# The second layer's w_in operands kept in DRAM as f32, and split into high and low parts after they are loaded

## The chip, the cores and the metric

The kernel runs on one core of one Trainium2 chip. The metric is device time in microseconds (us), the median of three runs. The engines are named as in the profile: PE (TensorE, the matmuls), PEld (its weight loads), DVE (VectorE), ACT (ScalarE), POOL (GpSimd), SP (SyncE, which here only issues DMA transfers).

## The reference, cut to what matters

Three stages follow each other: an attention over chunks of 32 queries, an MLP with softplus, and an MLP with PReLU, whose slope `alpha` is a vector over the 2048 hidden units. All is in float32.

```
a   = softmax(scale * q_c @ k_full.T)      # 24 chunks of 32 queries, 4 batches, 8 heads
x   = (a @ v_full)                         # laid out as 3072 tokens x 512
h   = x @ moe_w_in                         # 512 x 2048
x   = (relu(h) + log1p(exp(-|h|))) @ moe_w_out
h   = x @ moe2_w_in
out = (relu(h) + alpha * min(h, 0)) @ moe2_w_out
```

## The kernel before, in words

Matmuls run on f32r operands. To keep the accuracy of f32, each operand is split: the high part is a cast by ACT (`act.copy` into an f32r tile), the low part is the difference of the operand and its high part. A product is then three matmuls: high by high, high by low, low by high. In each group of three, the first two use the high part of the weight; the third alone uses its low part. The second alone uses the low part of the moving operand.

**First layer and attention.** Here every step of every engine is a piece with a cost, a due time and rooms that it takes and gives back. The class `Plan` orders the pieces for each engine, eight times over with refined due times, and the best order is written out. `raw` weights come in as 64-bit words, DVE turns them into f32 (`magnitude`, `clamp`, `convert`), and the second layer's weights are prepared along the way: for each q of 8, `weight_sums` lets POOL form four sums, then the seven operands (A11, A12, A22, S1 to S4, each 128x256) are split by ACT and POOL in a staging room (`wst`) and stored to DRAM by SP, high and low parts, in `in_ops`. Operands for w_out go the same way to `out_ops`.

**Second layer.** Three pairs of token blocks (p = 0, 1, 2) follow each other. A pair has eight quads (`quad`, q = 0 to 7), which compute h with seven products instead of eight, and then 56 groups (`second`, n = 0 to 55), which multiply by w_out. A quad has 42 matmuls in the order A11, S1, S2, S3, A12, S4, A22; a group has six. Each quad reads two rooms of `win`, loaded by `load_w_in` two quads ahead, behind the quad's last product. ACT and DVE take the products out of PSUM: copies c1 and c5 (tile `tc`), sums (`u`, `ps_q`, `gb`), the PReLU (`tp`, then `gb`). In the 56 groups, `ready` makes the moving operand `g`: a cast by ACT, a subtraction by DVE, three groups ahead at the end. The engines' queues are in program order. Rooms of `win` are shared with others (tag "w", 16 rooms).

At the end of the 56 groups, `second` loads the operands of the next pair's first two quads, one room each at 12, 8, 4 and 1 groups before the end; `flip` transposes results and stores them by four DMAs for each half.

Of the kernel before, what the change touches and what calls it, by code (L numbers as in the profile page):

```python
# [7 lines left out]
F32 = mybir.dt.float32  # L8
F32R = mybir.dt.float32r
I32 = mybir.dt.int32  # L10
AF = mybir.ActivationFunctionType
ALU = mybir.AluOpType
# [4 lines left out]
P = 128  # L17
DM, DFF = 512, 2048
# [32 lines left out]
NPAIRS = NB // 2  # L51
# [125 lines left out]
def attention_mlp_mlp_kernel(ctx: ExitStack, tc, qk, v, w1, w2, consts, out):  # L177
# [22 lines left out]
    ident = cst[:, :P]  # L200
    alpha_sb = cst[:, P:]
    y_dram = dpool.tile([DM, NTOK], F32, name="y_dram")
    in_ops = dpool.tile([NQ, P, 2, 7, HK], F32, name="in_ops")
    out_ops = dpool.tile([7, 2, P, NQ // 2, 2, HK], F32, name="out_ops")


# [90 lines left out]
        pool.tensor_tensor(out=t[:, 2, :], in0=a11, in1=a21, **sub)  # L297
        pool.tensor_tensor(out=t[:, 3, :], in0=a12, in1=t[:, 1, :], **sub)

    def operands_at(q, second, k, n):  # L300

        if second:
            return [out_ops[k + e, q // 4][:, q % 4] for e in range(n)]
        return [in_ops[q][:, :, k:k + n, :].rearrange("p a k n -> p a (k n)")]


    raw_q, q_t, k_t, v_t, st, s_room = {}, {}, {}, {}, {}, {}
# [264 lines left out]

    y_raw, x_op, w_in, w_out, slots, G, g2 = {}, {}, {}, {}, {}, {}, {}

    def switch_pools():
        early.close()
# [35 lines left out]
        t, x = y_raw.pop((p, h, k)), x_op[p, k][:, :, h, :]  # L614
        dve.tensor_tensor(out=x[:, 1, :], in0=t, in1=x[:, 0, :].bitcast(F32), op=ALU.subtract)

    def load_w_in(n, part=(0, 1)):
        if n >= NPAIRS * NQ:
            return
        p, q = divmod(n, NQ)  # L620
        for a, b in [((0, 4), (4, 7))[e] for e in part]:
            t = wpool.tile([P, 2, b - a, HK], F32R, tag="w", name="win")
            sp.dma_start(out=t.bitcast(F32), in_=in_ops[q][:, :, a:b, :])
            for k in range(a, b):
                w_in[n, k] = t[:, :, k - a, :]


    PASSES = ((S1, T1, 1), (A11, B11, 0), (S4, B22, 3), (S2, T2, 1), (S3, T3, 0), (A12, B21, 2), (A22, T4, 1))
# [51 lines left out]
    def plus(out, in0, in1, op=ALU.add):  # L680
        dve.tensor_tensor(out=out, in0=in0, in1=in1, op=op)
# [3 lines left out]
    def quad(p, q, between, ahead):  # L685


        n, f0, f1 = p * NQ + q, 2 * q, 2 * q + 1
        if q % 4 == 0:
            for k in range(4):  # L690
                room = (wpool if k else xpool).tile([P, 4, N2], F32, tag="w" if k else "x", name="gb")
                slots[k, q // 4] = room
                for e in range(4):
                    G[k, q + e] = room[:, e, :]
        banks = [("acc", ps_acc)] * 4 if q % 2 else [("pa", ps_a), ("h", ps_h)] * 2
        x1, x4, x3, x2 = (bank(space, tag) for tag, space in banks)
# [12 lines left out]
        ahead(2)
        n3 = negative(G[3, q], f1)  # L710
        between()
        product(p, n, A12, B21, x1, False)
        n0 = halves_of(x1, G[0, q])
        ahead(3)
        product(p, n, S4, B22, x4, False)
        prelu(G[3, q], n3, G[3, q])
        plus(G[1, q], x4, u2)
        minus_prelu(n0, f0, G[0, q])
        if q < NQ - 1:
            n1 = negative(G[1, q], f0)  # L720
        product(p, n, A22, T4, x3, False)

        def second_rest(n1):
            prelu(G[1, q], n1, G[1, q])
            dve.scalar_tensor_tensor(out=G[1, q], in0=G[1, q], scalar=-1.0, in1=G[0, q], op0=ALU.mult, op1=ALU.subtract)
        if q < NQ - 1:
            second_rest(n1)
            n2 = halves_of(x3, G[2, q])
            minus_prelu(n2, f1, G[2, q])
        else:  # L730
            third = []
            rest[:] = [
                lambda: second_rest(negative(G[1, q], f0)),
                lambda: third.append(halves_of(x3, G[2, q])),
                lambda: minus_prelu(third[0], f1, G[2, q]),
            ]
        if q < NQ - 2:
            load_w_in(n + 2)
        else:
            for k in range(2):  # L740
                load_w_out(14 * p + 2 * (q - NQ + 2) + k)

# [40 lines left out]
    def second(p, todo):  # L783
# [34 lines left out]
        for n in range(7 * NQ):  # L818
            i, q = divmod(n, NQ)
            ka = PASSES[i][0]  # L820
            w = w_out[14 * p + n // 4][:, n % 4]
            if q == 0:
                ps = ps_of[ka] = [bank(*spaces[ka]) for _ in range(2)] if ka in spaces else ps_of[A11]
            g = g2.pop(n)

            def products(m, ps=ps, w=w, g=g, q=q):
                for k, (a, e) in enumerate(((0, 0), (0, 1), (1, 0))):
                    pe.matmul(
                        ps[m], lhsT=w[:, a, m * P:(m + 1) * P], rhs=g[:, e, :], start=ka in spaces and q == 0 and k == 0,
                        stop=q == NQ - 1 and k == 2, skip_group_check=ka not in spaces,  # L830
                    )
            products(0)
            if p == NPAIRS - 1 and n >= 7 * NQ - 3:
                behind.append(products)
            else:
                products(1)
            if n % 4 == 3:
                w_out.pop(14 * p + n // 4)
                if n // 4 + 4 < 14:
                    load_w_out(14 * p + n // 4 + 4)  # L840
            if p == NPAIRS - 1:
                for at, k, e in ((4, 1, 3), (12, 0, 1), (26, 1, 2)):
                    if at <= n < at + NQ:
                        sums_now.append(lambda k=k, e=e, q=n - at: plus(G[k, q], G[k, q], G[e, q]))
            elif n in SUMS:
                half, k, e = SUMS[n]
                pool.dma_start(out=slots[k, half], in_=slots[e, half], accum_op=ALU.add)
            while asked[0] < min(7 * NQ, n + (5 if n < 3 else 4 if n < DEEP - 3 else 3)):
                ready(asked[0])
                asked[0] += 1  # L850
            if rest:
                rest.pop(0)()
            while sums_now:
                sums_now.pop(0)()
            if behind and n == 7 * NQ - 1:
                ending(ps, kept, behind)
                return None
            if q == NQ - 1:
                later = after(ka, ps)
                while i == 6 and later:  # L860
                    later.pop(0)()
            elif later:
                later.pop(0)()
            for at, half, d, b in ((39, 0, 0, 1), (39, 1, 0, 1), (46, 0, 1, 1), (46, 1, 1, 1), (50, 0, 0, 0), (51, 1, 0, 0)):
                if n == at:
                    flip(c[d, b], 2 * p + b, d, [half])
            for piece in todo.get(n, ()):
                piece()
            if 7 * NQ - n in (12, 8, 4, 1):
                k = (12, 8, 4, 1).index(7 * NQ - n)  # L870
                load_w_in((p + 1) * NQ + k // 2, (k % 2,))
        return lambda: flip(c.pop((1, 0)), 2 * p, 1)

    def prepare(p):
# [32 lines left out]
    def schedule(when):  # L907
# [136 lines left out]
        for j in range(4 * NQ):  # L1044
# [20 lines left out]
            if e % 2:  # L1065
                z, k0 = e // 2, 4 * q + e // 2
                add(("sums2", q, z), "POOL", 3.4, due + 3, lambda q=q, z=z: weight_sums(q, z),
                    [("cv2", j)] + ([("sl2", q - (not z), 1 - z, 4)] if j > 1 else []), ["raw"])

                wide, narrow = (k0 + 2 * z, k0 + 2 - 2 * z)  # L1070
                part = slice(0, HK) if z else slice(HK, DM)
                split_task((q, z, 0), lambda k=wide: words[1, k], DM, operands_at(q, z, A12 if z else A11, 2), [("sums2", q, z)], 1.4, ["word"])
                split_task((q, z, 1), lambda k=narrow, part=part: words[1, k][:, part], HK, operands_at(q, z, A11 if z else A22, 1), [("sl2", q, z, 0)], 0.9, ["word"])
                for n in (0, 2):
                    split_task((q, z, 2 + n), lambda q=q, z=z, n=n: sums[q, z][:, n:n + 2, :], DM, operands_at(q, z, S1 + n, 2),
                               [("sl2", q, z, 1 + n)], 1.4, ["raw"] if n else [])
                    if n == 0:
                        add(("sl2", q, z, 3), "", 0, 0, lambda: None, [("sl2", q, z, 2)])

        add("switch", "", 0, 0, switch_pools, [("xl", t) for t in range(NT)])  # L1080
        for h in range(2):
# [4 lines left out]
            for n, k in enumerate(order_y):  # L1086
# [3 lines left out]
                    after = [("y4", h)]  # L1090
                add(("yo", h, k), "ACT", 0.62, due + 10 + 2 * n, lambda h=h, k=k: high_y(0, h, k), after, ["w"] if not h and k > 1 else [])
                add(("yd", h, k), "DVE", 0.72, due + 11 + 2 * n, lambda h=h, k=k: low_y(0, h, k), [("yo", h, k)], [], ["y"])
        dma(("win0",), 1.0, 4.8, when[last], lambda: load_w_in(0), [("yo", 0, T4)], ["w"] * 2)
        dma(("win1",), 1.0, 4.8, when[last], lambda: load_w_in(1), [("i", "win0")], ["w"] * 2)

        plan.run()
        return plan
# [83 lines left out]
```

## Time and profile before

| what | value |
|---|---|
| median of 3 runs | 1091.12 us (1090.8 to 1093.66) |
| span of the profiled execution, first to last instruction | 1088.6 us |
| PE busy | 1064.7 us, 98% |
| DVE, ACT, POOL busy | 715.6, 559.0, 231.2 us |
| first matmul of the second layer, of its second and third pair | 623.01, 778.06, 930.73 us |

The profile gives no time of the profiled execution other than its span, which is 2.5 us under the median; the rest lies before the first and behind the last instruction. Every instruction has the line L71, that of a helper, so that instructions are told apart by the tiles they write and read.

### The profile page before, as it was taken

The page shows a single profiled execution, that of the slowest core. Times are in us where ns is not written, and L with a number is a line of the kernel's source. Part 1 is how long each engine was busy: PE and PEld are TensorE (multiplying, and loading weights), DVE is VectorE, ACT ScalarE, POOL GpSimd, SP SyncE. Part 2 cuts the span into 40 slices and gives each one's busy share as a digit, 9 for nine tenths or more (in the row PEclk, how much of TensorE's full clock was granted, in tenths as well). Part 3 has the DMA queues.
Part 4 walks back from the last instruction along what each step waited for, and adds up shares of the span by engine and source line. Part 5 has one row for each costly group of instructions (what it writes and reads, how often), then busy time and mean ns, then how long its engine had stood idle before and what let it go on. Part 6 is the DMA issues. An engine that isn't in the chain of part 4 may idle for free.

```text
span 1088.6 us, 16448 instructions
## 1 busy us (share of the span) xinstructions
PE 1064.7 (98%) x5999; PEld 873.6 (80%) x6003; DVE 715.6 (66%) x1150; ACT 559.0 (51%) x974; POOL 231.2 (21%) x281
## 2 busy tenths in 40 slices
PE   6789999999999999999999999999999999999998
PEld 4578878888888888888888888888888888888886
DVE  6789989566744554454358156678666779566976
ACT  5654335565553554353244355664555755456643
POOL 4434434334222332223233400000000000000000
PEclk9999999999999999999999999999999999999999
DMA  9955574658644565444356373799874999856904
GB/s 227 226 154 173 170 190 129 172 170 207 173 143 155 158 188 139 171 123 145 107 201 229 132 289 125 283 280 323 199 278 174 329 299 256 251 209 251 377 1 78
DMA packets 173840, 214.55 MB, mean 197 GB/s; under 512 B 96064, under 2 KB 125888, under 8 KB 166848
## 3 DMA queue, kind: packets, MB, share of 16 engines
q1 hardware_dynamic: 169456, 196.59, 56.7%
q0 software_dynamic: 4032, 16.78, 7.8%
q8 instruction: 48, 0.79, 0.3%
q14 instruction: 32, 0.26, 0.1%
q10 hardware_dynamic: 272, 0.13, 0.0%
HBM read 154.74 MB, written 46.14 MB: 185 GB/s over the span
## 4 chain that ended last, share of the span: by engine, by line
PE 91%; DVE 3%; DMA 2%; issue 1%; SPq 1%; ACT 1%; POOL 0%; DVEq 0%; ACTq 0%; POOLq 0%
PE ps_q L71 42%; PE ps_o L71 23%; PE ps_hh L71 22%; DVE word L71 2%; PE ps_x L71 2%; PE ps_s L71 2%; DMA raw<-in_w_dram 1%; PE ps_t L71 1%; DMA qk<-in_qk_dram 1%; SPq L71 1%; DMA v<-in_v_dram 0%; ACT pt L71 0%; DVE sm L71 0%; DVE o_sb L71 0%; DVE g L71 0%
## 5 line engine op out<-in xcount | busy, mean ns | idle before, releaser
L71 PE MATMUL ps_hh<-x,wsplit 128*128 128x512 f32 x1152 | 281.1, 393 | 0.3 <-DVE x L71 0.2
L71 PE MATMUL ps_o<-g,wsplit 128*128 128x512 f32 x1152 | 279.1, 391 | 0.8 <-ACT ta L71 0.7
L71 PEld LDWEIGHTS ps_o<-g,wsplit 128*128 128x128 f32 x1152 | 214.8, 188 | 46.5 <-ACT ta L71 1.1
L71 PEld LDWEIGHTS ps_hh<-x,wsplit 128*128 128x128 f32 x1152 | 215.3, 189 | 45.5 <-DVE x L71 0.5
L71 PE MATMUL ps_q<-g,wout 128*128 128x512 f32 x1008 | 229.3, 389 | 0.0
L71 PE MATMUL ps_q<-xop,win 128*128 128x512 f32 x1008 | 229.1, 389 | 0.0
L71 PEld LDWEIGHTS ps_q<-g,wout 128*128 128x128 f32 x1008 | 189.0, 188 | 39.8 <-ACT gb L71 0.5
L71 PEld LDWEIGHTS ps_q<-xop,win 128*128 128x128 f32 x1008 | 189.2, 188 | 39.3
L71 DVE TENSOR_TENSOR g<-ta,g 128x512 fp32r<-128x512 f32 x96 | 71.2, 742 | 132.0 <-ACT g L71 131.8
L71 ACT CAST g<-gb 128x512 fp32r<-128x512 f32 x168 | 100.9, 622 | 89.6 <-PE ps_q L71 64.2
L71 DVE TENSOR_TENSOR g<-gb,g 128x512 fp32r<-128x512 f32 x168 | 114.0, 686 | 35.5 <-ACT g L71 33.6
L71 ACT CAST g<-ta 128x512 fp32r<-128x512 f32 x96 | 59.6, 621 | 147.5 <-PE ps_o L71 147.3
L71 ACT ACTIVATE ta<-ps_hh 128x512 f32<-128x512 f32 x96 | 57.4, 598 | 106.4 <-PE ps_hh L71 106.0
L71 DVE SCALAR_TENSOR_TENSOR word<-raw,word 128x512 int32<-128x512 int32 x128 | 104.6, 818 | 2.5
L71 ACT ACTIVATE tp<-gb 128x512 f32<-128x512 f32 x48 | 30.4, 633 | 91.8 <-DVE gb L71 91.8
L71 POOL TENSOR_TENSOR wst<-wsum,wst 128x512 fp32r<-128x512 f32 x32 | 42.1, 1316 | 122.4 <-ACT wst L71 122.3
L71 DVE TENSOR_SCALAR word<-word 128x512 f32<-128x512 f32 (+1 forms) x128 | 66.1, 521 | 1.8
L71 POOL DMA_DIRECT2D gb<-gb x12 | 10.5, 872 | 264.2 <-DVE g L71 183.0
L71 POOL TENSOR_TENSOR wsplit<-word,wsplit 128x512 fp32r<-128x512 f32 x32 | 48.9, 1530 | 64.4 <-ACT wsplit L71 64.2
L71 DVE TENSOR_SCALAR word<-raw 128x512 int32<-128x512 int32 x64 | 38.1, 597 | 36.8 <-DMA raw<-in_w_dram 23.8
L71 DVE SCALAR_TENSOR_TENSOR gb<-gb,tp 128x512 f32<-128x512 f32 x48 | 33.2, 691 | 44.0 <-ACT tp L71 44.0
L71 POOL TENSOR_TENSOR wst<-word,wst 128x512 fp32r<-128x512 f32 (+1 forms) x32 | 36.6, 1145 | 113.4 <-ACT wst L71 113.4
(81 smaller groups left out, 926.0 us busy)
## 6 DMA issues: line engine op xcount, KB each, us to landing
wout<-out_ops SPq DMA_DIRECT2D x42, 1024.0 KB
raw<-in_w_dram SPq DMA_DIRECT2D x64, 512.0 KB
win<-in_ops SPq DMA_DIRECT2D x24, 1024.0 KB
win<-in_ops SPq DMA_DIRECT2D x24, 768.0 KB
out_ops<-wst SPq DMA_DIRECT2D x56, 256.0 KB
in_ops<-wst SPq DMA_DIRECT2D x24, 512.0 KB
gb<-gb POOLq DMA_DIRECT2D x12, 1024.0 KB, 13.3
v<-in_v_dram SPq DMA_DIRECT2D x48, 128.0 KB
```

What stands on the lines that cost most here:

```text
L71: i = getattr(self.engine, name)(*args, **kw)
```

## The change

The operands of w_in are kept in DRAM as f32, half the bytes: `in_ops` loses its dimension of 2, and the first layer stores words and sums as they are, without a cast, a subtraction or a staging room. In the second layer, `load_w_in` loads the f32 operands into the low half of the room, ACT casts them into the high half (`high_w_in`), and POOL subtracts in place (`low_w_in`). The two rooms of a quad now hold A11, S1, S2, S3 (part 0) and A12, S4, A22 (part 1). Part 0 of the quad after the next is loaded at the start of a quad, part 1 behind S3. Both parts of the next quad are split behind S1, which is in the program order behind c5. For a pair's first quad the splits stand 6 and 3 groups before the end of the 56 groups before it.

```diff
-    in_ops = dpool.tile([NQ, P, 2, 7, HK], F32, name="in_ops")
+    in_ops = dpool.tile([NQ, P, 7, HK], F32, name="in_ops")
...
+    def store_in(q, n):
+
+        to, f0, f1 = in_ops[q], words[1, 4 * q], words[1, 4 * q + 2]
+        if n == 0:
+            sp.dma_start(out=to[:, 0:5:4, :], in_=f0.rearrange("p (k n) -> p k n", k=2))
+        elif n == 1:
+            sp.dma_start(out=to[:, 6, :], in_=f1[:, HK:])
+        elif n == 2:
+            sp.dma_start(out=to[:, 1:4, :], in_=sums[q, 0][:, 0:3, :])
+        else:
+            sp.dma_start(out=to[:, 5, :], in_=sums[q, 0][:, 3, :])
...
+    IN_PARTS = ((A11, S1, S2, S3), (A12, S4, A22))
+
+    def load_w_in(n, part):
         if n >= NPAIRS * NQ:
             return
-        p, q = divmod(n, NQ)
-        for a, b in [((0, 4), (4, 7))[e] for e in part]:
-            t = wpool.tile([P, 2, b - a, HK], F32R, tag="w", name="win")
-            sp.dma_start(out=t.bitcast(F32), in_=in_ops[q][:, :, a:b, :])
-            for k in range(a, b):
-                w_in[n, k] = t[:, :, k - a, :]
+        q, keys = n % NQ, IN_PARTS[part]
+        t = w_raw[n, part] = wpool.tile([P, 2, len(keys), HK], F32R, tag="w", name="win")
+        sp.dma_start(out=t[:, 1].bitcast(F32), in_=in_ops[q][:, 4 * part:4 * part + len(keys), :])
+        for k, key in enumerate(keys):
+            w_in[n, key] = t[:, :, k, :]
+
+    def high_w_in(n, part):
+        t = w_raw[n, part]
+        act.copy(out=t[:, 0], in_=t[:, 1].bitcast(F32))
+
+    def low_w_in(n, part):
+        t = w_raw.pop((n, part))
+        pool.tensor_tensor(out=t[:, 1], in0=t[:, 1].bitcast(F32), in1=t[:, 0].bitcast(F32), op=ALU.subtract)
+
+    def split_w_in(n, part):
+        if n < NPAIRS * NQ:
+            high_w_in(n, part)
+            low_w_in(n, part)
...
+        if q < NQ - 2:
+            load_w_in(n + 2, 0)
...
         c5 = copy(x4, "tl")
         ahead(1)
+        if q < NQ - 1:
+            for part in range(2):
+                split_w_in(n + 1, part)
         product(p, n, S2, T2, x2, True)
...
         product(p, n, S3, T3, x3, True)
+        if q < NQ - 2:
+            load_w_in(n + 2, 1)
...
-        if q < NQ - 2:
-            load_w_in(n + 2)
-        else:
+        if q >= NQ - 2:
...
             if 7 * NQ - n in (12, 8, 4, 1):
                 k = (12, 8, 4, 1).index(7 * NQ - n)
-                load_w_in((p + 1) * NQ + k // 2, (k % 2,))
+                load_w_in((p + 1) * NQ + k // 2, k % 2)
+            if 7 * NQ - n in (6, 3):
+                split_w_in((p + 1) * NQ, int(7 * NQ - n == 3))
```

The planner's pieces follow: four stores for each q in place of four splits, and for the first quad two casts ("wq") and two subtractions ("wd"). Since pieces are gone, the planner orders the rest of the first layer anew; on PE the first 172 of 359 rows (a row is a run of like instructions) are the same, and behind it the same pieces follow in a slightly different order.

The first place is ACT at the end of a pair's 56 groups (here the first pair's), where the last casts of `g` stand. Before:

```order
L71 CAST g<-gb 128x512
L71 ACTIVATE c<-ps_q 128x512
L71 CAST xop<-yt 128x512
L71 CAST g<-gb 128x512
L71 ACTIVATE c<-ps_q 128x512
L71 CAST g<-gb 128x512 x4
L71 COPY tc<-ps_q 128x512 x2
L71 ACTIVATE tp<-gb 128x512
```

And with the change:

```order
L71 CAST g<-gb 128x512
L71 ACTIVATE c<-ps_q 128x512
L71 CAST xop<-yt 128x512
L71 CAST g<-gb 128x512
L71 ACTIVATE c<-ps_q 128x512
L71 CAST g<-gb 128x512
L71 CAST win<-win 128x1024
L71 CAST g<-gb 128x512 x3
L71 CAST win<-win 128x768
L71 COPY tc<-ps_q 128x512 x2
L71 CAST win<-win 128x1024
L71 CAST win<-win 128x768
```

The cast of part 0 of the next pair's first quad now stands ahead of the last three casts of `g`, that of part 1 behind them; the two casts behind `tc` are those of the second quad, inside the first.

The second place is ACT in a quad in the middle of a pair, from the copies of `tc` (c1 and c5) on. Before:

```order
L71 COPY tc<-ps_q 128x512 x2
L71 ACTIVATE tp<-gb 128x512
L71 ACTIVATE tp<-tp,cst 128x512
L71 ACTIVATE tp<-ps_q 128x512
L71 ACTIVATE gb<-ps_q 128x512
```

And with the change:

```order
L71 COPY tc<-ps_q 128x512 x2
L71 CAST win<-win 128x1024
L71 CAST win<-win 128x768
L71 ACTIVATE tp<-gb 128x512
L71 ACTIVATE tp<-tp,cst 128x512
L71 ACTIVATE tp<-ps_q 128x512
L71 ACTIVATE gb<-ps_q 128x512
```

Two casts stand between the copies and the first step of the PReLU (`tp<-gb`).

The third place is POOL over the second layer, whose only instructions before were twelve DMA issues that add one half of `gb` to another. Before:

```order
L71 TENSOR_TENSOR wst<-wsum,wst 128x512 x2
L71 DMA gb<-gb 128x2048 x12
```

And with the change, from the first pair's last quads to the second pair's first:

```order
L71 TENSOR_TENSOR win<-win 128x1024
L71 TENSOR_TENSOR win<-win 128x768
L71 DMA gb<-gb 128x2048 x6
L71 TENSOR_TENSOR win<-win 128x1024
L71 TENSOR_TENSOR win<-win 128x768
L71 TENSOR_TENSOR win<-win 128x1024
```

Two subtractions for each quad stand in POOL's queue, those of the second pair's first quad right behind the DMA issues.

## Rows read from the trace of the kernel before

**Rows 1.** The page: the span, its first part, and the slices of PE.

```profile
span 1088.6 us, 16448 instructions
PE 1064.7 (98%) x5999; PEld 873.6 (80%) x6003; DVE 715.6 (66%) x1150; ACT 559.0 (51%) x974; POOL 231.2 (21%) x281
PE   6789999999999999999999999999999999999998
```

**Rows 2.** The chain that ended last, its two longest pieces: start, length, engine, count.

```profile
631.33 223.74 PE ps_q L71 x987
855.11 228.15 PE ps_q L71 x1005
```

**Rows 3.** Whom PE waited for, one of its rows: total us, times, longest.

```profile
PE ps_o L71 <- ACT ta L71: 0.7, 1, 0.7
```

**Rows 4.** Groups of instructions by form: count, busy us, mean ns, idle before.

```profile
L71 DVE TENSOR_TENSOR g<-gb,g 128x512 fp32r<-128x512 f32 x168 | 114.0, 686 | 35.5 <-ACT g L71 33.6
...
L71 DVE TENSOR_TENSOR g<-ta,g 128x512 fp32r<-128x512 f32 x96 | 71.2, 742 | 132.0 <-ACT g L71 131.8
...
L71 ACT CAST g<-gb 128x512 fp32r<-128x512 f32 x168 | 100.9, 622 | 89.6 <-PE ps_q L71 64.2 <-DVE g L71 20.6 <-DMA out_dram<-c 4.4
...
L71 ACT CAST wst<-word 128x256 fp32r<-128x256 f32 x16 | 6.4, 402 | 2.0 <-DMA out_ops<-wst 1.5 <-DMA in_ops<-wst 0.5
```

**Rows 5.** Timeline of POOL in the first layer: start, us, instruction, idle before.

```profile
185.46 0.74 POOL L71 TENSOR_TENSOR wsum<-word 128x256 f32<-128x256 f32 x1 [3.10 <-DVE sm L71]
186.28 1.06 POOL L71 TENSOR_TENSOR wsum<-wsum,word 128x256 f32<-128x256 f32 x1
...
224.39 0.73 POOL L71 TENSOR_TENSOR wst<-word,wst 128x256 fp32r<-128x256 f32 x1 [3.95 <-ACT wst L71]
228.04 1.29 POOL L71 TENSOR_TENSOR wst<-wsum,wst 128x512 fp32r<-128x512 f32 x1 [2.91 <-ACT wst L71]
```

**Rows 6.** Timeline of DVE beside it.

```profile
185.62 1.13 DVE L71 TENSOR_TENSOR g<-ta,g 128x512 fp32r<-128x512 f32 x1
186.67 1.22 DVE L71 TENSOR_TENSOR s_sb<-s_sb,r 128x512 f32<-128x512 f32 x1
```

**Rows 7.** Timeline of ACT in the second pair's second quad and after.

```profile
794.75 0.63 ACT L71 ACTIVATE tp<-gb 128x512 f32<-128x512 f32 x1 [3.45 <-DVE gb L71]
...
797.49 0.64 ACT L71 ACTIVATE tp<-gb 128x512 f32<-128x512 f32 x1 [0.39 <-DVE gb L71]
...
799.75 1.07 ACT L71 COPY tc<-ps_q 128x512 f32<-128x512 f32 x2
```

**Rows 8.** Timeline of DVE in the same quad.

```profile
796.17 0.69 DVE L71 SCALAR_TENSOR_TENSOR gb<-gb,tp 128x512 f32<-128x512 f32 x1 [1.45 <-ACT tp L71]
```

**Rows 9.** Timelines of SP, ACT, DVE and PE at the end of the first pair.

```profile
764.73 0.52 SPq L71 DMA_DIRECT2D win<-in_ops  x1
...
770.10 0.62 ACT L71 CAST g<-gb 128x512 fp32r<-128x512 f32 x1
...
772.12 0.69 DVE L71 TENSOR_TENSOR g<-gb,g 128x512 fp32r<-128x512 f32 x1
...
778.06 54.11 PE L71 MATMUL ps_q<-xop,win 128*128 128x512 f32 x238
```

**Rows 10.** Timelines of ACT and PE at the end of the second pair.

```profile
923.05 0.61 ACT L71 CAST g<-gb 128x512 fp32r<-128x512 f32 x1
...
930.73 3.56 PE L71 MATMUL ps_q<-xop,win 128*128 128x512 f32 x15
```

**Rows 11.** Timelines of SP and DVE, two loads.

```profile
779.52 1.18 SPq L71 DMA_DIRECT2D win<-in_ops  x2
...
186.46 0.45 SPq L71 DMA_DIRECT2D raw<-in_w_dram  x1
...
191.32 0.43 DVE L71 TENSOR_SCALAR word<-raw 128x512 int32<-128x512 int32 x1 [1.59 <-DMA raw<-in_w_dram]
```

More of the change, by code (lines that the diff above doesn't have):

```diff
@@ L298, in weight_sums, with out_at @@
         pool.tensor_tensor(out=t[:, 3, :], in0=a12, in1=t[:, 1, :], **sub)
[L300 to L304, printed above, removed]
+    def out_at(q, k, n):
+        return [out_ops[k + e, q // 4][:, q % 4] for e in range(n)]
+    def store_in(q, n):
[8 more added lines that the diff above has]
+            sp.dma_start(out=to[:, 5, :], in_=sums[q, 0][:, 3, :])
     raw_q, q_t, k_t, v_t, st, s_room = {}, {}, {}, {}, {}, {}
@@ L567, in pe_out @@
             drain(acc.pop(b), b)
-    y_raw, x_op, w_in, w_out, slots, G, g2 = {}, {}, {}, {}, {}, {}, {}
+    w_raw, y_raw, x_op, w_in, w_out, slots, G, g2 = {}, {}, {}, {}, {}, {}, {}, {}
     def switch_pools():
@@ L615, in low_y @@
         dve.tensor_tensor(out=x[:, 1, :], in0=t, in1=x[:, 0, :].bitcast(F32), op=ALU.subtract)
-    def load_w_in(n, part=(0, 1)):
+    IN_PARTS = ((A11, S1, S2, S3), (A12, S4, A22))
+    def load_w_in(n, part):
         if n >= NPAIRS * NQ:
             return
-        p, q = divmod(n, NQ)
-        for a, b in [((0, 4), (4, 7))[e] for e in part]:
-            t = wpool.tile([P, 2, b - a, HK], F32R, tag="w", name="win")
-            sp.dma_start(out=t.bitcast(F32), in_=in_ops[q][:, :, a:b, :])
-            for k in range(a, b):
-                w_in[n, k] = t[:, :, k - a, :]
+        q, keys = n % NQ, IN_PARTS[part]
[13 more added lines that the diff above has]
+            low_w_in(n, part)
     PASSES = ((S1, T1, 1), (A11, B11, 0), (S4, B22, 3), (S2, T2, 1), (S3, T3, 0), (A12, B21, 2), (A22, T4, 1))
@@ L1068, in schedule @@
                     [("cv2", j)] + ([("sl2", q - (not z), 1 - z, 4)] if j > 1 else []), ["raw"])
[L1070 to L1073, printed above, removed]
+                if z == 0:
+                    for n, give in enumerate((["word"], ["word"], [], [])):
+                        dma(("ss2", q, 0, n), 0.45, (1.0, 0.5, 1.5, 0.5)[n], due + 6, lambda q=q, n=n: store_in(q, n), [("sums2", q, 0)], [], give)
+                    add(("sl2", q, 0, 4), "", 0, 0, nothing, [("sums2", q, 0)])
+                    add(("sg2", q), "", 0, 0, nothing, [("ss2", q, 0, 2), ("ss2", q, 0, 3)], [], ["raw"])
+                    continue
+                split_task((q, 1, 0), lambda k=k0 + 2: words[1, k], DM, out_at(q, A12, 2), [("sums2", q, 1)], 1.4, ["word"])
+                split_task((q, 1, 1), lambda k=k0: words[1, k][:, :HK], HK, out_at(q, A11, 1), [("sl2", q, 1, 0)], 0.9, ["word"])
                 for n in (0, 2):
-                    split_task((q, z, 2 + n), lambda q=q, z=z, n=n: sums[q, z][:, n:n + 2, :], DM, operands_at(q, z, S1 + n, 2),
-                               [("sl2", q, z, 1 + n)], 1.4, ["raw"] if n else [])
+                    split_task((q, 1, 2 + n), lambda q=q, n=n: sums[q, 1][:, n:n + 2, :], DM, out_at(q, S1 + n, 2),
+                               [("sl2", q, 1, 1 + n)], 1.4, ["raw"] if n else [])
                     if n == 0:
-                        add(("sl2", q, z, 3), "", 0, 0, lambda: None, [("sl2", q, z, 2)])
+                        add(("sl2", q, 1, 3), "", 0, 0, nothing, [("sl2", q, 1, 2)])
         add("switch", "", 0, 0, switch_pools, [("xl", t) for t in range(NT)])
@@ L1092, in schedule @@
                 add(("yd", h, k), "DVE", 0.72, due + 11 + 2 * n, lambda h=h, k=k: low_y(0, h, k), [("yo", h, k)], [], ["y"])
-        dma(("win0",), 1.0, 4.8, when[last], lambda: load_w_in(0), [("yo", 0, T4)], ["w"] * 2)
-        dma(("win1",), 1.0, 4.8, when[last], lambda: load_w_in(1), [("i", "win0")], ["w"] * 2)
+        for n in range(4):
+            dma(("win", n), 0.5, 1.9, when[last], lambda n=n: load_w_in(n // 2, n % 2), [("i", "win", n - 1)] if n else [("yo", 0, T4)], ["w"])
+            if n < 2:
+                add(("wq", n), "ACT", 1.1, when[last] + 6, lambda n=n: high_w_in(0, n), [("win", n)])
+                add(("wd", n), "POOL", 2.6, when[last] + 7, lambda n=n: low_w_in(0, n), [("wq", n)])
         plan.run()
```

## The prediction

> **What bounds the kernel now.** First the page: PE is busy for 1064.7 of 1088.6 us, and its slices show that the 24 us without it lie in the first four, that is before 109 us [rows 1]. Then the chain that ended last: through the whole second layer it is PE alone, 987 matmuls in 223.74 us, then 1005 in 228.15, which is 226.7 and 227.0 ns each [rows 2]. Nothing stops PE there; a quad of 42 matmuls lasts 9.52 us, a group of six 1.36. Then the list of whom PE waited for: behind the start its longest wait is one of 0.7 us for ACT [rows 3]. So work that is taken from ACT, POOL, SP or DMA behind 109 us buys at most that 0.7 us. The question is only whether the work that the change puts into the second layer ever makes PE wait.
>
> **The first layer.** Out go, for each of eight q, three casts and three subtractions of 128x512 and one each of 128x256. By 622 and 402 ns [rows 4] that is 2.27 us of ACT for each q, 18 in all; by 1.29 and 0.73 us [rows 5] 4.6 us of POOL, 37 in all. Half the bytes stored and loaded go too. All of it lies beside PE, so I count 0. The casts and stores taken out come behind the start; the orders of PE, DVE, ACT and SP are the same ahead of them, so the 24 us stay. Behind that, PE's order has the same adjacencies: 16 single blocks of transposes, 14 of scores next to values, six of either alone, before and now. I count 0 for the new order, and keep a rival for it.
>
> **The splits, priced.** ACT: 402 ns for 256 columns and 622 for 512 give 220 for each 256 more, so 1.06 us for 1024 and 0.84 for 768 [rows 4]. POOL: 0.73 and 1.29 us give 0.56 for each 256 more, so 2.41 and 1.85 [rows 5]. These forms don't stand in the trace. For the long one the bounds are one instruction of 512 columns and two of them (0.62 to 1.24 us on ACT, 1.29 to 2.58 on POOL); I take the straight line, which lies near the upper end, since both engines' times grow with the columns. In 24 quads that is 46 us of ACT and 102 of POOL, far from either engine's limit.
>
> **What POOL does to DVE.** The rows to read are those where both work. A DVE subtraction with both inputs in SBUF began at 185.62, 0.16 us behind a POOL sum that ran to 186.20, and took 1.13 us where its kind takes 0.69 [rows 4 to 6]. The next DVE instruction began at 186.67 and took 1.22, and the POOL sum that began at 186.28 took 1.06 instead of 0.74 [rows 5, 6]. Read so, each of the two waits until the other's instruction has ended, and they take turns. The mean says less: 742 ns for `g` beside a POOL that is partly busy, 686 without [rows 4]; that is 56 ns of an average, and with it alone nothing below would be late. I take the single rows, since a subtraction of 2.41 us is a longer block than any that the mean contains. The Trainium skill ("SBUF — State Buffer", Who interferes with whom) has a rule that speaks against this change: a VectorE instruction with two SBUF inputs and a GpSimd one that reads SBUF exclude each other, and the second to issue is fully blocked until the first has finished. By that rule the sum comes out as below, by the mean it would be 0; the single rows agree with the rule.
>
> **In the middle of a pair.** The quad that began at 797.10 (778.06 plus two quads) had its copies c1 and c5 end at 800.82, 3.72 us into it, and ACT then waited 3.45 us for `gb` in the quad before [rows 7]. The two casts take 1.9 of these 3.45. POOL: part 0 from 4.85 to 7.26 us into the quad, part 1 to 9.15. Part 0's low part is first read by the third matmul of the next quad, at 9.52 + 0.45 = 9.97: 2.7 us to spare. Part 1's is read four products later. The first two-input DVE instruction in the way is `gb<-gb,tp`, at 796.17, that is 8.59 into its quad [rows 8]: it waits until 9.15, 0.56 us. What is late next: c1 and c5 of the next quad, by the same 0.56. c1 ends at 3.2 us into its quad, and PE wants its bank again at 5.44, for product A12: 2.2 us to spare. So here I count 0; the cover is that reserve.
>
> **At the end of a pair.** Here the cover is thin. ACT casts part 0 of the next pair's first quad ahead of the last three casts of `g`. Its load was issued at 764.73 [rows 9]; a load of the same size took 4.9 us from issue to DVE's use [rows 11], so it is there at 769.6. The cast begins when that of `g` at 770.10 is through, 770.72 to 771.78 [rows 9]. POOL subtracts from 771.85 to 774.26. DVE's subtraction for the third `g` from the end ran at 772.12 before [rows 9]; its cast now ends at about 772.4, so POOL holds the way, and it runs from 774.26 to 774.95. PE's group for it begins three groups ahead of 778.06 [rows 9], at 773.98, and reads the low part in its second matmul, at 774.21. So PE waits 0.74 us. The next `g` follows by 1.25 us (a transpose lies between), in time for a group 1.36 later.
>
> The same at the end of the second pair: cast at 923.05 [rows 10], so the part is cast by 924.73, subtracted by 927.2, `g` by 927.9; PE wants it at 930.73 - 4.08 + 0.23 = 926.88: 1.02 us. Part 1, cast behind the last `g`, finds no two-input DVE instruction before it ends. Two ends of pairs: 1.76 us. The first pair's first quad is split during the first layer.
>
> **The second quad of a pair.** Its load was issued at 779.52; with the 4.9 us of the load above it is there at 784.4 [rows 11], behind c5. ACT casts it to 785.5, and POOL is done by 787.9. PE reads it at 778.06 + 9.97 = 788.03, plus the 0.74 that PE is late already: in time, and I count 0. If it lands 2 us later, behind the stores of `flip`, it costs 1.1 us for each of two pairs, within the range.
>
> **Sum.** 1088.6 + 1.76 = 1090.4 for the span. The median lies 2.5 us above the span, so 1091.12 + 1.76 = 1092.9 us. A run of this kernel can tell about 0.3% (3.3 us) from no change, so this is no change.
>
> **Rivals.** (1) POOL hardly blocks DVE, as the mean has it: no wait at the ends of pairs, 1091.1. For it speaks that mean; against it the single rows.
>
> (2) Slower: the block feeds back. `gb<-gb,tp` waits for part 1, then PReLU, c1, c5, the casts and POOL of the next quad follow. From 796.17 to the end of c5 at 800.82 it is 4.65 us [rows 7, 8], and the casts and subtractions up to the end of part 1 add 1.06 + 0.07 + 2.41 + 1.85 + 0.05 = 5.44: 10.09 for a turn, against 9.52 for a quad. If POOL always goes first, each quad is 0.57 later; after four the 2.2 us are used up, and the other three splitting quads of each of three pairs cost 0.57 each, 5.1 us: 1092.9 + 5.1 = 1098.0. Against it: from a lag of 1.5 us on, `gb<-gb,tp` is ready 0.3 us before part 0 ends, and the two took turns in the rows, so it slips between the parts and the lag falls back. It decides whether DVE gets that turn.
>
> (3) The new order of the first layer goes wrong in a place: the planner's prices are its own, and the two subtractions of the first quad (2.41, 1.85) also lie in the way of `g`, whose reserve there is about 1.3 us. One such block costs at most 1.1 us; several late tiles of attention 3 to 5: 1094 to 1098. For it: the order is new from 185 us on; against it: before, the same planner left PE no wait beyond 0.7 us there.
>
> (4) A gain: the 0.7 us wait goes and nothing is late, 1090.4.
>
> **Chances and range.** The forecast, with 0.5 to 3 us of waits, 0.57; (1) 0.18; (2) 0.10; (3) 0.11; (4) 0.04. Faster by over 0.3% would need 3.3 us, of which only 0.7 can be found behind the start: 0.04, for a start that comes out otherwise. Slower by over 0.3%, that is over 1094.4: all of (2), half of (3), and a little of the forecast, 0.19. The same: 0.77. The range takes in (1) and (4) below, from 1090.3, and on the other side a half of (2) or (3), to 1096.0.
>
> **What would show it.** Right: on PE, two waits of 0.5 to 1.3 us, three groups ahead of the second and third pair, ended by DVE `g`, beside a POOL subtraction of 128x1024 of about 2.4 us; no wait of PE inside quads; `gb<-gb,tp` on DVE longer than 0.69 us in quads; ACT's casts of `win` of about 1.06 and 0.84 us. Wrong: no lengthened DVE instruction beside POOL (rival 1); waits of PE for ACT `tc` or DVE in the fifth product of the later quads of a pair (rival 2); waits for attention or `g` between 185 and 623 us (rival 3); a first matmul of the second layer away from 623.

## The result, and the profile after

The changed kernel takes 1097.44 us (median of 1094.36, 1099.45, 1097.59 and 1097.3), the kernel before, beside it, 1091.86. The ratio is 1.0051, 95% interval 1.0031 to 1.0071: slower by half a per cent, and outside the predicted range.

The page, where [rows 1] stood: busy time of each engine, over a span of 1092.6 us.

```profile
PE 1066.0 (98%) x5999; PEld 871.5 (80%) x6003; DVE 725.6 (66%) x1150; ACT 583.9 (53%) x990; POOL 293.7 (27%) x297
```

DVE's share is as before, ACT's and POOL's are a little higher, and none of the three is near its limit; PE's is 98% still. PE's timeline in the second layer tells where the time went (start, length of the stretch, and in brackets PE's idle time just ahead, with what ended it):

```profile
620.55 5.60 PE L71 MATMUL ps_q<-xop,win 128*128 128x512 f32 x24
625.99 2.88 PE L71 MATMUL ps_o<-g,wsplit 128*128 128x512 f32 x12
628.71 69.52 PE L71 MATMUL ps_q<-xop,win 128*128 128x512 f32 x306
698.74 1.65 PE L71 MATMUL ps_q<-xop,win 128*128 128x512 f32 x6 [0.51 <-DVE gb L71]
700.23 72.83 PE L71 MATMUL ps_q<-g,wout 128*128 128x512 f32 x319
773.46 3.02 PE L71 MATMUL ps_q<-g,wout 128*128 128x512 f32 x12 [0.40 <-DVE g L71]
776.91 1.43 PE L71 MATMUL ps_q<-g,wout 128*128 128x512 f32 x5 [0.43 <-DVE g L71]
778.18 74.97 PE L71 MATMUL ps_q<-xop,win 128*128 128x512 f32 x330
853.89 1.65 PE L71 MATMUL ps_q<-xop,win 128*128 128x512 f32 x6 [0.75 <-DVE gb L71]
...
1009.07 1.66 PE L71 MATMUL ps_q<-xop,win 128*128 128x512 f32 x6 [0.76 <-DVE gb L71]
1010.57 76.67 PE L71 MATMUL ps_q<-g,wout 128*128 128x512 f32 x336
1087.08 1.45 PE L71 MATMUL ps_q<-cst,c 128*128 128x128 f32 x8
```

Two kinds of waits are new: for `gb`, ahead of the last product (A22) of each pair's last quad, and twice for `g` at the end of the first two pairs. The bracket is less than the lateness, because the ends of matmuls are modelled; starts tell it better. Eight quads begin to begin take 76.16 us when nothing stops them (78.88 in the first pair, where 12 matmuls of the first layer lie between), and so do 56 groups. Differences of such starts give this table, the measure for all that follows:

| kernel | first, second, third pair: quads | groups | second layer |
|---|---|---|---|
| before | 78.88, 76.17, 76.16 | 76.17, 76.50, 76.19 | 460.07 |
| after | 79.68, 77.20, 77.24 | 77.95, 77.95, 76.51 | 466.53 |

That is 6.46 us, against 5.6 between the medians (3.4 to 7.8 by the ratio's interval). The second layer's begin can't be used so: its first matmul lay at 620.55 us here and at 623.01 before, and it scattered from 620.35 to 624.89 over the experiments below, whose first layers are that of the changed kernel (in six of them, POOL's two subtractions for the first quad differ). All of that scatter comes from the start. A run of PE near 109 us shows it, before and then after:

```profile
109.54 2.97 PE L71 MATMUL ps_o<-g,wsplit 128*128 128x512 f32 x12
```

```profile
107.05 2.99 PE L71 MATMUL ps_o<-g,wsplit 128*128 128x512 f32 x12
```

From there to the second layer it is 513.47 us before, 513.50 after, and 513.47 to 513.54 in the twelve experiments. The wait of [rows 3] is in the list after the change, too:

```profile
PE ps_o L71 <- ACT ta L71: 0.7, 1, 0.7
```

**In the quads.** DVE's first `gb` from `gb` and `tp` in a quad [rows 8], and POOL's two subtractions, one run of 4.21 us, in the first pair:

```profile
641.38 0.69 DVE L71 SCALAR_TENSOR_TENSOR gb<-gb,tp 128x512 f32<-128x512 f32 x1 [1.46 <-ACT tp L71]
650.90 0.93 DVE L71 SCALAR_TENSOR_TENSOR gb<-gb,tp 128x512 f32<-128x512 f32 x1 [1.46 <-ACT tp L71]
...
679.46 1.64 DVE L71 SCALAR_TENSOR_TENSOR gb<-gb,tp 128x512 f32<-128x512 f32 x1 [1.46 <-ACT tp L71]
...
686.83 0.69 DVE L71 TENSOR_TENSOR gb<-ps_q,tc 128x512 f32<-128x512 f32 x1
688.98 1.86 DVE L71 SCALAR_TENSOR_TENSOR gb<-gb,tp 128x512 f32<-128x512 f32 x1 [1.46 <-ACT tp L71]
```

```profile
637.32 4.21 POOL L71 TENSOR_TENSOR win<-win 128x1024 fp32r<-128x1024 f32 x2 [8.03 <-ACT win L71]
647.06 4.22 POOL L71 TENSOR_TENSOR win<-win 128x1024 fp32r<-128x1024 f32 x2 [5.53 <-ACT win L71]
...
686.08 4.21 POOL L71 TENSOR_TENSOR win<-win 128x1024 fp32r<-128x1024 f32 x2 [5.53 <-ACT win L71]
```

DVE's instruction begins every 9.52 us, with the quads; POOL begins every 9.74 to 9.79, five steps in 48.76. So POOL ends 0.22 us or a little more later in each quad, and DVE's instruction always ends 0.55 us behind POOL's last: 651.28 and 651.83, 690.29 and 690.84. It grows from 0.69 to 1.86 us. Its neighbour `gb<-ps_q,tc` at 686.83, with one input in PSUM, lay wholly under POOL's subtraction and took 0.69.

In the last quad this lag of 1.17 us meets DVE's order: two subtractions for `g` stand ahead of the third sum, which frees A22's bank (the part of PSUM to which that product adds). DVE before, and then after:

```profile
697.17 0.69 DVE L71 TENSOR_TENSOR g<-gb,g 128x512 fp32r<-128x512 f32 x1 [0.29 <-ACT g L71]
697.78 0.68 DVE L71 TENSOR_TENSOR u<-ps_q,tc 128x512 f32<-128x512 f32 x1
698.56 0.70 DVE L71 TENSOR_TENSOR ps_q<-ps_q,u 128x512 f32<-128x512 f32 x1
699.30 0.69 DVE L71 TENSOR_TENSOR gb<-ps_q,tc 128x512 f32<-128x512 f32 x1
```

```profile
695.87 0.69 DVE L71 TENSOR_TENSOR g<-gb,g 128x512 fp32r<-128x512 f32 x1 [0.28 <-ACT g L71]
696.47 0.68 DVE L71 TENSOR_TENSOR u<-ps_q,tc 128x512 f32<-128x512 f32 x1
697.26 0.70 DVE L71 TENSOR_TENSOR ps_q<-ps_q,u 128x512 f32<-128x512 f32 x1
698.00 0.69 DVE L71 TENSOR_TENSOR gb<-ps_q,tc 128x512 f32<-128x512 f32 x1
```

Before, the quad began at 692.37 (623.01 + 78.88 - 9.52) and wanted the bank at its A22, 8.16 later, 700.53; `gb` ended at 699.99, 0.54 us ahead. After, it began at 689.91 and would have wanted it at 698.07; `gb` ended at 698.69. PE came to A22 at 698.74, 0.67 late.

**At the end of a pair** (DVE, POOL and ACT, where [rows 9] stood):

```profile
770.92 2.48 DVE L71 TENSOR_TENSOR g<-gb,g 128x512 fp32r<-128x512 f32 x1 [0.15 <-ACT g L71]
773.33 0.70 DVE L71 STREAM_TRANSPOSE c<-c 128x512 f32<-128x512 f32 x1
773.96 2.90 DVE L71 TENSOR_TENSOR g<-gb,g 128x512 fp32r<-128x512 f32 x2
```

```profile
770.46 2.40 POOL L71 TENSOR_TENSOR win<-win 128x1024 fp32r<-128x1024 f32 x1 [27.86 <-ACT win L71]
774.31 2.00 POOL L71 TENSOR_TENSOR win<-win 128x768 fp32r<-128x768 f32 x1 [1.45 <-ACT win L71]
```

```profile
769.33 1.05 ACT L71 CAST win<-win 128x1024 fp32r<-128x1024 f32 x1
770.28 0.61 ACT L71 CAST g<-gb 128x512 fp32r<-128x512 f32 x1
771.52 1.14 ACT L71 CAST g<-gb 128x512 fp32r<-128x512 f32 x2 [0.63 <-PE ps_q L71]
773.34 0.83 ACT L71 CAST win<-win 128x768 fp32r<-128x768 f32 x1 [0.68 <-DMA win<-in_ops]
```

The third `g` from the end took 2.48 us, to 0.54 behind POOL's part 0. That made the last two late: 2.90 us for two that take 1.3 otherwise, since part 1 came between them. Part 1's cast waited for its load and for nothing else, so the load's landing decides which `g` it meets.

### The profile page after: what moved, and what is told of

Read it like the earlier page. It is cut to its first block, busy times and chain, and to the rows that moved or that the text cites. A ratio compares the mean times of both kernels' runs of the same rounds, so it can differ in the third digit from the quotient of the medians.

```text
span 1092.6 us, 16496 instructions
## 1 busy us (share of the span) xinstructions
PE 1066.0 (98%) x5999; PEld 871.5 (80%) x6003; DVE 725.6 (66%) x1150; ACT 583.9 (53%) x990; POOL 293.7 (27%) x297
## 4 chain that ended last, share of the span: by engine, by line
PE 87%; DMA 4%; ACT 3%; DVE 3%; SPq 2%; issue 1%; DVEq 0%; ACTq 0%
PE ps_q L71 35%; PE ps_o L71 24%; PE ps_hh L71 23%; SPq L71 2%; DMA qk<-in_qk_dram 2%; PE ps_x L71 2%; ACT tp L71 2%; DVE gb L71 2%; PE ps_s L71 1%; DMA v<-in_v_dram 1%; PE ps_t L71 1%; DVE g L71 1%; DMA raw<-in_w_dram 1%; ACT tc L71 0%; DVE ps_q L71 0%
## 5 line engine op out<-in xcount | busy, mean ns | idle before, releaser
L71 POOL TENSOR_TENSOR win<-win 128x1024 fp32r<-128x1024 f32 (+1 forms) x48 | 102.1, 2147 | 252.3 <-ACT win L71 234.3
L71 DVE TENSOR_TENSOR g<-gb,g 128x512 fp32r<-128x512 f32 x168 | 120.8, 727 | 36.4 <-ACT g L71 34.4
L71 DVE SCALAR_TENSOR_TENSOR word<-raw,word 128x512 int32<-128x512 int32 x128 | 101.9, 797 | 2.5
L71 DVE SCALAR_TENSOR_TENSOR gb<-gb,tp 128x512 f32<-128x512 f32 x48 | 46.0, 958 | 44.0 <-ACT tp L71 44.0
L71 DVE TENSOR_SCALAR word<-word 128x512 f32<-128x512 f32 (+1 forms) x128 | 61.8, 487 | 2.0
L71 POOL TENSOR_TENSOR wsum<-word 128x256 f32<-128x256 f32 x32 | 26.5, 828 | 87.1 <-DVE word L71 70.7
```

What stands on the lines that cost most here:

```text
L71: i = getattr(self.engine, name)(*args, **kw)
```

## The experiments

Theory 1: a long subtraction on POOL keeps DVE's instructions with two inputs in SBUF waiting. Rivals: it is POOL's total time and not the length of one instruction (1b); the casts in ACT's order (2); late loads (3). The first four edits:

```diff
 low_w_in, x1_no_low:
-        pool.tensor_tensor(out=t[:, 1], ...)
 low_w_in, x2_pieces and x4_pieces_late:
-        pool.tensor_tensor(out=t[:, 1], in0=t[:, 1].bitcast(F32), ...)
+        for k in range(t.shape[2]):
+            pool.tensor_tensor(out=t[:, 1, k], in0=t[:, 1, k].bitcast(F32), ...)
 second, x3_late and x4_pieces_late:
-            if 7 * NQ - n in (6, 3):
-                split_w_in((p + 1) * NQ, int(7 * NQ - n == 3))
+            if 7 * NQ - n in (3, 1):
+                split_w_in((p + 1) * NQ, int(7 * NQ - n == 1))
```

**x1_no_low.** 

> Leaves out POOL's subtraction of win, so the low half of the room keeps the loaded f32 and the output is not the reference's; ACT's casts and the loads stay. The measure is the second layer, from its first matmul to the first transpose of the last results: 460.1 us before, 466.5 after. Theory 1 (POOL's long subtractions keep DVE's subtractions of two SBUF inputs waiting): about 460.2 us, no PE wait for DVE, median about 1091.9. Theory 2 (the extra casts stand in ACT's queue and make the rest late): stays near 466 us and 1097. Theory 3 (the loads land late): likewise near 466.

**x2_pieces.** 

> POOL subtracts in pieces of 256 columns, 7 instructions a quad of about 0.73 us instead of 2.41 and 1.89, so 5.1 us of POOL a quad instead of 4.3. Theory 1 with turn-taking (what counts is the length of one POOL instruction): DVE is held up for at most 0.73 us, the first gb from tp stays under 1.45 us and doesn't grow over the quads, PE's waits for DVE at the ends of pairs go; second layer 460 to 461.5 us, median about 1092. Theory 1b (POOL's total time counts): drift and waits as in the changed kernel or worse, 466 us or more, 1097 or more. Theory 2: 466.

**x3_late.** 

> At the end of a pair, the splits of the next pair's first quad stand behind the last casts of g instead of ahead of the last three and behind the last one. Theory 1: the 3.6 us of waits at the two pair ends go, the waits of 0.67 to 0.94 us in the last quads stay: second layer about 463, median about 1094.3; unless the split is now late for the quad's third matmul, then a wait for POOL win of up to 2 us at the start of the pair. Theory 2: ACT's casts out of the way of g also take the 3.6 us away, so this run parts 1 and 2 only together with the first.

**x4_pieces_late.** 

> Pieces of 256 columns and the later place at the end of a pair together. Theory 1 with turn-taking: no wait of PE in the second layer above 0.3 us, 460.2 us, median about 1091.9, the kernel of before. Theory 1b (POOL's total counts): the waits in the quads stay or grow, 463 us or more. Theory 2: the quads' waits stay, about 463.

| kernel | quads | groups | second layer | ratio to before |
|---|---|---|---|---|
| x1_no_low | 78.88, 76.16, 76.16 | 76.18, 76.16, 76.21 | 459.75 | 1.0000 (0.9988 to 1.0011) |
| x2_pieces | 78.88, 76.16, 76.16 | 76.20, 76.32, 76.42 | 460.14 | 0.9993 (0.9982 to 1.0003) |
| x3_late | 79.72, 77.25, 77.22 | 76.54, 76.51, 76.52 | 463.76 | 1.0033 (1.0022 to 1.0044) |
| x4_pieces_late | 78.87, 76.16, 76.16 | 76.22, 76.30, 76.32 | 460.03 | 0.9999 (0.9989 to 1.0009) |

x1_no_low keeps every cast and load and has no wait: theories 2 and 3 fall, all 6.5 us come from POOL's subtractions. x2_pieces has more POOL work than the changed kernel, yet no wait either: 1b falls. x3_late takes 2.8 us away, not 3.6, and leaves the waits for `gb`. DVE's and POOL's groups in the second layer of x2_pieces show both sides of the exchange (busy time, then the mean in ns of one):

```profile
L71 DVE SCALAR_TENSOR_TENSOR gb<-gb,tp 128x512 f32<-128x512 f32 x48 | 38.0, 793 | 42.9 <-ACT tp L71 42.9
L71 POOL TENSOR_TENSOR win<-win 128x256 fp32r<-128x256 f32 x161 | 127.6, 829 | 180.7 <-ACT win L71 168.7 <-issue 12.1
```

The mean of `gb` falls from 958 ns in the changed kernel to 793 (its longest is 1.29 us), and POOL's pieces take 829 in the mean where 0.73 us [rows 5] was read for one: POOL now waits as well.

The next four ask what in POOL's work blocks, how long a piece may be, and which place in the order each wait needs.

```diff
 low_w_in, x5_memset:
+        for _ in range(2):
+            pool.memset(t[:, 1].bitcast(F32), 0.0)
 low_w_in, x7_halves:
+        for k in range(0, t.shape[2], 2):
+            b = min(k + 2, t.shape[2])
+            pool.tensor_tensor(out=t[:, 1, k:b], in0=t[:, 1, k:b].bitcast(F32), ...)
 quad, x8_g_behind (ahead(0) and ahead(1) only for q < NQ - 1 in their old places):
         plus(G[3, q], x3, c5)
+        if q == NQ - 1:
+            ahead(0)
+            ahead(1)
         ahead(2)
 second, x10_part1_late:
-            if 7 * NQ - n in (6, 3):
+            if 7 * NQ - n in (6, 1):
```

**x5_memset.** 

> In place of each subtraction POOL fills the low half of the room with zeros, twice, in the same place of its order; it leaves out the low part of w_in. POOL then works for a time that should be near that of the subtraction, but reads nothing from SBUF. By the rule that only a POOL instruction that reads SBUF excludes a DVE one with two inputs in SBUF: no DVE instruction is lengthened (gb from gb and tp 0.69 us, g 0.69), second layer about 460.1 us. If any long POOL work on the room blocks DVE: gb from tp lengthened, and 462 to 466.5 us, as far as a fill is as long as a subtraction.

**x7_halves.** 

> Pieces of 512 columns (1.29 us; the last one of part 1 0.73). If the length of one POOL instruction is what counts: DVE held for at most 1.29 us, gb from tp never above 2.0 us and in the mean between 0.79 (pieces of 256) and 0.96 (long ones); at the ends of pairs a wait of PE of at most 0.3 us; second layer 460.1 to 461 us. If POOL's total counts: about 466.

**x8_g_behind.** 

> The long subtractions stay. In the last quad of a pair, the casts and subtractions of the first two g stand behind the third sum (u, ps_q, gb) instead of ahead of it. If the waits in the last quad come from a lag that has grown over six quads (0.22 us each) and meets the two g in DVE's order: the lag stays (gb from gb and tp grows from 0.69 to about 1.9 us over the quads as before), the three waits for gb of 0.67 to 0.94 us and the 0.35 us behind them go, the ends of pairs keep theirs: second layer about 463 us. If the lag alone made gb late: no change, 466.5.

**x10_part1_late.** 

> At the end of a pair, part 0 is split where the change has it (six groups ahead), part 1 one group before the end instead of three. If each of the two POOL subtractions there blocks one g: the wait three groups ahead of the pair (1.15 us) stays, the one in the last group (0.4 us in the timeline, some 0.7 of lateness) goes, at both pair ends: second layer 465 to 465.7 us. If the second wait is only the rest of the first: 466.5.

| kernel | quads | groups | second layer | ratio to before |
|---|---|---|---|---|
| x5_memset | 78.88, 76.16, 76.16 | 76.18, 76.18, 76.20 | 459.76 | 0.9989 (0.9978 to 1.0001) |
| x7_halves | 78.88, 76.16, 76.16 | 76.42, 76.20, 76.18 | 460.00 | 0.9999 (0.9986 to 1.0013) |
| x8_g_behind | 78.88, 76.20, 76.19 | 76.84, 77.87, 76.19 | 462.17 | 1.0022 (1.0009 to 1.0035) |
| x10_part1_late | 79.75, 77.28, 77.25 | 77.94, 78.73, 76.53 | 467.48 | 1.0053 (1.0032 to 1.0073) |

x5_memset: the length alone proves little, since two fills (0.96 and 0.74 us each) are over before `gb` comes. The end of the pair decides; POOL and DVE there:

```profile
769.50 1.98 POOL L71 MEMSET win<- 128x1024 f32 x2 [27.83 <-ACT win L71]
```

```profile
769.99 0.69 DVE L71 TENSOR_TENSOR g<-gb,g 128x512 fp32r<-128x512 f32 x1 [0.15 <-ACT g L71]
```

The `g` lay wholly under POOL's fill and took 0.69 us: POOL's writing doesn't block.

x7_halves: pieces of 512 columns are short enough, with no wait of PE in the list; the longest `gb` took 1.21 us, the mean, 780 ns, is just under the band expected.

x8_g_behind: the lag stays (0.93, 1.15, 1.35, 1.67, 1.92 us in the first pair) and the waits for `gb` go, so lag and order together made them. The first pair's end cost only 0.7 us; there the load landed later, ACT waited 1.30 us for it, and POOL's part 1 began when the last `g` was running:

```profile
773.56 1.97 POOL L71 TENSOR_TENSOR win<-win 128x768 fp32r<-128x768 f32 x1 [2.07 <-ACT win L71]
```

```profile
772.58 1.25 DVE L71 TENSOR_TENSOR g<-gb,g 128x512 fp32r<-128x512 f32 x2
```

x10_part1_late missed: neither the expected gain nor no change, but 1 us more. The edit moves part 1 behind nothing on ACT, where the last `g` was cast already; the cast still waits for the load. At the second pair's end that landed a little earlier, and POOL went in ahead of both last `g` instead of between them:

```profile
932.06 1.83 POOL L71 TENSOR_TENSOR win<-win 128x768 fp32r<-128x768 f32 x1 [1.03 <-DMA out_dram<-c]
```

```profile
932.12 2.92 DVE L71 TENSOR_TENSOR g<-gb,g 128x512 fp32r<-128x512 f32 x2
```

DVE was 0.06 us too late, and PE waited 1.21 us. At the ends of pairs, ACT, DVE, POOL and SP have the orders of the changed kernel, so the 0.95 us between 467.48 and 466.53 shows how far the same order can scatter, and the edit could not tell the two blocks apart. Of the last four edits, one asks whether one input from SBUF is enough to block, two leave out one of the blocks at the ends of pairs, and one tries the account as a whole.

```diff
 low_w_in, x9_copy:
+        pool.tensor_copy(out=t[:, 1], in_=t[:, 0].bitcast(F32))
 low_w_in, x11_no_low1_at_ends (x12_no_low0_at_ends: part == 0):
+        if n in (NQ, 2 * NQ) and part == 1:
+            return
 x13_order_only: the edits of x8_g_behind and x3_late
```

**x9_copy.** 

> In place of each subtraction POOL copies the high half of the room to the low half: one input, read from SBUF; it leaves out the low part of w_in. The fills with zeros, which read nothing, lengthened no DVE instruction and gave 459.8 us. If a read from SBUF is what excludes, however many inputs: gb from tp is lengthened wherever a copy is running when it begins; with a copy nearer to a fill (0.96 and 0.74 us) than to a subtraction (2.4 and 1.9) the block is short, and the second layer is 460 to 461.5 us. If it takes two inputs on POOL as well: no lengthened instruction, 459.8.

**x11_no_low1_at_ends.** 

> POOL's subtraction of part 1 is left out for the first quads of the second and third pair alone (their operands A12, S4, A22 keep a wrong low half). If it is what makes PE wait a second time at each pair end: the waits of 1.15 us three groups ahead stay, the second ones go, the last quads' waits stay: second layer about 465.2 us. If the second wait comes from the first block alone: 466.5.

**x12_no_low0_at_ends.** 

> POOL's subtraction of part 0 is left out for the first quads of the second and third pair alone (their A11, S1, S2, S3 keep a wrong low half). The g are then on time, and part 1's subtraction, which begins when its load has landed and been cast, comes behind the last g: both waits go, the last quads' waits stay, second layer 463.4 to 463.9 us. If part 1's block does not hang on part 0's: about 0.6 us more at each end, 464.8.

**x13_order_only.** 

> All of POOL's long subtractions stay, and two places alone move: the first two g behind gb in the last quad, and the splits at the end of a pair behind the last casts of g. If the account is whole (lag meets the g in the last quad; POOL meets the last g at the ends of pairs), gb from tp still grows to about 1.9 us over the quads, and PE waits nowhere in the second layer: 460.1 to 460.5 us, the time of before. If something else of the subtractions costs time as well: above 461.

| kernel | quads | groups | second layer | ratio to before |
|---|---|---|---|---|
| x9_copy | 78.88, 76.16, 76.16 | 76.16, 76.18, 76.18 | 459.72 | 0.9996 (0.9984 to 1.0007) |
| x11_no_low1_at_ends | 79.72, 77.21, 77.18 | 77.18, 77.20, 76.52 | 465.01 | 1.0036 (1.0023 to 1.0050) |
| x12_no_low0_at_ends | 79.70, 77.21, 77.22 | 76.52, 76.51, 76.56 | 463.72 | 1.0025 (1.0015 to 1.0035) |
| x13_order_only | 78.88, 76.16, 76.16 | 76.16, 76.42, 76.16 | 459.94 | 0.9996 (0.9983 to 1.0008) |

x9_copy's second layer is as short as if it took two inputs on POOL to block, but its copies, too, are over before `gb` comes, so the quads decide nothing. At the end of the pair, POOL and DVE:

```profile
772.21 1.04 POOL L71 CAST win<-win 128x1024 fp32r<-128x1024 f32 x1 [27.84 <-ACT win L71]
```

```profile
772.69 1.10 DVE L71 TENSOR_TENSOR g<-gb,g 128x512 fp32r<-128x512 f32 x1 [0.15 <-ACT g L71]
```

The `g` ended 0.54 us behind the copy, as it did behind subtractions: one input read from SBUF is enough to block.

x11 and x12 part the ends of pairs: without any block the 56 groups take 76.52 and 76.51 us, with part 0's alone 77.18 and 77.20, with both 77.95 and 77.95. So the first costs 0.67 us at each end and the second 0.76, and the second needs the first. x13_order_only closes the account: POOL's subtractions are as long as in the changed kernel (2402 and 1850 ns in the mean), `gb` still grows to 1.86 us in the first pair, and PE's list has no wait in the second layer:

```profile
629.83 70.88 PE L71 MATMUL ps_q<-xop,win 128*128 128x512 f32 x312
700.55 76.32 PE L71 MATMUL ps_q<-g,wout 128*128 128x512 f32 x336
776.71 76.32 PE L71 MATMUL ps_q<-xop,win 128*128 128x512 f32 x336
```

## Why the prediction was wrong, step by step

**What bounds, and the first layer: right.** PE is the bound. Behind its start the first layer takes 513.50 us against 513.47, and where the second layer is as long as before, so is the kernel, within the intervals of 0.1% (x1_no_low 1.0000, x13_order_only 0.9996). Two details were off: the 24 us at the start don't stay, since the run near 109 us begins anywhere from 106.83 to 111.37 us in the fourteen traces; and "Nothing stops PE there" passed over the break between the two pieces of [rows 2], a wait of which more below.

**The prices: right.** ACT's casts took 1070 and 853 ns in the mean against 1.06 and 0.84 us, POOL's subtractions 2405 and 1889 against 2.41 and 1.85.

**"In the middle of a pair": this step failed.** It counted 0, under cover of "that reserve", the 2.2 us ahead of product A12. The wait of DVE was seen, but priced for a single quad. The loop of rival 2 runs: from the end of `gb` to POOL's next begin 4.98 us (681.10 to 686.08), POOL 4.21, `gb` 0.55 behind it, together 9.74, not 10.09. The difference is the cast, which begins before the copy ahead of it has ended, 0.11; 0.05 of POOL; and 0.19, since a blocked instruction ends 0.55 us behind its blocker and not 0.74. The prediction's own rows had that 0.55: the first DVE instruction of [rows 6] ended at 186.75, POOL's at 186.20. So the loop gained 0.22 us on each quad, not 0.57. The reason against it was that `gb` would slip between the two parts "from a lag of 1.5 us on". In the seventh quad, part 0 ended at 688.48 (686.08 + 2.40) and `gb` began at 688.98: another 0.5 us of lag was wanted, more than two quads, and the pair was over.

Nor was the cover 2.2 us. What decides is A22 in the last quad, where DVE has two `g` in front of the third sum: 0.54 us, which no row of the prediction held. Of the 6.46 us this step cost 2.9 in the quads (0.80, 1.03, 1.08), and another 0.34 us behind each wait, in the first groups of w_out. PE's list doesn't name that part, but the list of its weight loads does, and so do the timelines of PEld and ACT behind the first wait:

```profile
PEld ps_q L71 <- ACT gb L71: 1.4, 3, 0.5
```

```profile
701.13 1.92 PEld L71 LDWEIGHTS ps_q<-g,wout 128*128 128x128 f32 x9 [0.48 <-ACT gb L71]
```

```profile
698.72 0.63 ACT L71 ACTIVATE tp<-gb 128x512 f32<-128x512 f32 x1 [2.37 <-DVE gb L71]
...
700.49 0.59 ACT L71 ACTIVATE gb<-ps_q 128x512 f32<-128x512 f32 x1
```

It is the same late `gb` once more: ACT's PReLU step on it stands ahead of the step that reads another bank out (`gb<-ps_q`, to 701.08), and the fourth matmul of the 56 groups, due three matmuls of 0.227 us behind the first at 700.23, that is at 700.91, waits for that step until 701.13. That is 0.22 us; the rest comes right behind it, since the matmuls next to a wait follow each other a little more slowly (12 in a row take 3.02 us behind a wait and 2.88 undisturbed). Behind the first and third pair this part goes with the wait for `gb` (x8_g_behind, x13_order_only). Behind the second, 0.26 us stays in x13_order_only, and before the change 0.33 us stood there, at the break in [rows 2]:

```profile
855.11 3.04 PEld L71 LDWEIGHTS ps_q<-g,wout 128*128 128x128 f32 x14 [0.46 <-ACT gb L71]
```

**"At the end of a pair": right in kind, too short.** The first block came where it was worked out: 0.67 us at both ends, where the sum had 0.74 and 1.02. But "part 1, cast behind the last `g`, finds no two-input DVE instruction before it ends" failed: the block of part 0 had itself made the last two `g` late, by some 1.8 us (2.48 less 0.69), and so brought them under part 1, 0.76 us at each end. The step looked for what part 1 meets in the order of before, and not in the order that part 0 leaves. Together 2.9 us instead of 1.76.

**The second quad's load: right**; PE has no wait in the second quad of a pair.

**The sum.** 2.9 in the quads, 3 times 0.34 behind them, 2 times 0.67 and 2 times 0.76 at the ends make 6.79, less the 0.33 that stood there before: 6.46, all of it. These terms are differences of the same tables, so that they add up proves little; the proof is x13_order_only, which keeps POOL's work and takes away both meetings. Rival 2's 1098.0 lay near the measured time by luck: its loop was more than twice too fast, and it had PE wait at another product.

**The turn-taking: right.** The single rows, and not the mean, were the ones to trust, so rival 1 falls; rivals 3 and 4 fall with the first layer. The Trainium skill ("SBUF — State Buffer", Who interferes with whom) says that a DVE instruction with two SBUF inputs contends with a GpSimd one that reads SBUF and not with one that only writes it, nor, outside the modes in which DVE uses two ports, does a DVE instruction with at most one SBUF input contend. The runs agree: 0.69 us beside a fill, 1.10 beside a copy, 0.69 for `gb<-ps_q,tc` beside a subtraction.

## What to carry to other kernels

When work is added to an engine that excludes another, follow the block over several turns of the loop and not over one: if the turn is longer than the period, the lag grows until the loop's last iteration, and the least reserve there, with what else stands in that engine's order, is the one that counts. Then go through the order once more with the first block in it, since what is late now meets what it did not meet before. The remedy is cheap: the same POOL work in pieces of 512 columns or less, or the same long pieces with two places moved, cost nothing that the intervals of 0.1% show.

## What the runs showed of the hardware that was not expected

A blocked DVE instruction ends 0.54 to 0.55 us behind the end of its POOL blocker, less than the 0.69 us that it takes alone, whether the blocker is a subtraction or a copy; [rows 5, 6] had it already. Who goes first is decided within hundredths: 0.06 us at one pair end was worth 0.8 us to PE. And the begin of the second layer scatters over 4.5 us (620.35 to 624.89), all of it from the first 112 us: from PE's run near 109 us on, it comes 513.47 to 513.54 us later in all fourteen traces. So a single span can't show a change of half a per cent, while the length of the second layer came out within 0.5 us (459.72 to 460.14) in all seven kernels without these waits.
